# Chunked attention and a quadratic-ReLU FFN: q and k of the first two tiles loaded as eight tokens per row, turned by quarter-array products, and the first loads in another order

## The chip, the cores and the metric

The kernel runs on one core of one Trainium2 chip. The core has five engines with instruction queues of their own: TensorE (PE in the profile, with PEld for its weight loads), VectorE (DVE), ScalarE (ACT), GpSimd (POOL) and SyncE (SP), which here only issues DMAs. Sixteen DMA engines move the data. The metric is the device time of one execution in microseconds; lower is better.

## The reference, cut to what matters

```python
# q, k, v: (8 batches, 8 heads, 576 tokens, 64), float32
q_c = q.reshape(B, H, 9, 64, 64)                     # chunks of 64 tokens, k and v likewise
scores = (1 / sqrt(64)) * q_c @ k_c.transpose(0, 1, 2, 4, 3)
attn = softmax(scores, axis=-1)                      # within each chunk only
out = attn @ v_c                                     # (B, H, S, 64)
x = out.transpose(0, 2, 1, 3).reshape(4608, 512)     # heads side by side
h = x @ w_in                                         # w_in  (512, 2048), float64
g = where(h >= 1, h, where(h <= -1, 0, (h + 1)**2 / 4))
return (g @ w_out).astype(float32)                   # w_out (2048, 512), float64
```

Attention is local to chunks of 64 tokens, so a chunk of a head is a 64 x 64 problem. The weights are float64 in memory.

## The kernel before, in words

The 4608 tokens are nine tiles of 512 (`T`), tile `t`. Eight tiles are the first 512 tokens of a batch; the fifth collects the last 64 tokens of all batches. For each tile there are four head pairs `g` (`NP`), each on 128 partitions, two heads of 64, and 16 blocks `j` (`NF`) of 128 FFN columns.

For a head pair, `load_heads` brings q, k and v; `attn_turn` turns q and k so that the 64 head dimensions lie on partitions; `scores_of` makes 32 products of 64 x 64, each on a quarter of TensorE's array; `attn_softmax` does the softmax on VectorE, ScalarE and, in the first tile, GpSimd; `attn_turn_back` turns the result e; `values_of` makes 32 more quarter products; and `attn_split` writes x into a high and a low part (`xh`, `xl`) for products in a reduced format. Tiles 0 and 1 (`t < FLIPPED`) turn on TensorE: `flip` makes four 128 x 128 transposes into PSUM and ScalarE copies the result out. Later tiles turn on VectorE in blocks of 32.

The FFN makes 12 products per block into h (`ffn_in`, line 554), the activation on ScalarE and VectorE, a split of the result (`ffn_split`) and 12 products back (`ffn_out`, line 589), two blocks later. Each of the 32 weight pieces (`wi` and `wo`, 512 KB each) is loaded once (`load_weight`) and turned from float64 words into a high and a low part by `prepare`: three steps on ScalarE (lines 271, 277, 296) and four on VectorE (lines 274, 281, 286, 300).

The order of the instructions is not that of the calls. Each call adds parts to a `Plan` with an engine, a cost, what it reads and writes, and for DMAs a `lag` and a time `moving`. `Plan.emit` then goes through a modelled time: on each engine, among the parts whose inputs are ready by the model, the part that was added first goes next. Each engine carries out its instructions in that order on the chip and waits where an input is not there. Where TensorE would be idle by the model before the first FFN products, unneeded products with the identity (`warm`, line 704) are put in.

SP issues nearly all loads in the plan's order; the two loads of k for the first two head pairs of tile 0 are issued by ScalarE's queue. `first_loads` (line 619) is the order of the first loads. `load_rows` brings q or k of tiles 0 and 1 in two DMAs of 128 KB, one per head: partition p gets token p of each of the eight chunks, so each piece that is contiguous in memory has 64 floats, 256 bytes. `load_values` brings v in pieces of that size for all tiles.

Of the kernel before, what the change touches and what calls it, by code (L numbers as in the profile page):

```python
# [140 lines left out]
def kernel(  # L141
# [15 lines left out]
    nc = tc.nc  # L157

    B, H, S, D = q.shape
# [3 lines left out]
    C = 64  # L163
    Q = 32
    NP = H // 2
    T = 512
    CT = T // C
    HALF = T // 2
# [137 lines left out]
    def heads_rows(src, t, h):  # L306


        if BATCH[t] is not None:
            return src[BATCH[t], h, :T, :].rearrange("(c p) d -> c p d", p=C)  # L310
        return src[:, h, T:, :]

    def load_rows(dst, src, t, g, queue):

        dst = dst.rearrange("p (c d) -> p c d", d=D)
        for j in range(2):
            queue.dma_start(
                out=dst[j * C:(j + 1) * C],
                in_=heads_rows(src, t, 2 * g + j).rearrange("c p d -> p c d"),
            )  # L320

    def load_blocks(dst, src, t, g, queue):
# [33 lines left out]
    def load_heads(t, g, which="qkv"):  # L356
        for n, src, bufs in (("q", q, q_bufs), ("k", k, k_bufs), ("v", v, v_bufs)):
            if n not in which:
                continue
            key, dst = room(n, bufs, t, g)  # L360
            load = load_values if n == "v" else load_rows if t < FLIPPED else load_blocks
            parts = 4 if load == load_blocks else 2
            if BATCH[t] is None:
                parts *= 2

            issuer, queue = ("act", nc.scalar) if (n, t) == ("k", 0) and g < 2 else ("sp", nc.sync)
            plan.add(
                issuer, 0.67 * parts,
                lambda load=load, dst=dst, src=src, queue=queue: load(dst, src, t, g, queue),
                (), (key,), lag=2.1, moving=2.2 if load == load_blocks else 1.2,  # L370
            )

    def flip(ps, src):
        for u in range(NS):
            cols = slice(u * P, (u + 1) * P)
            nc.tensor.transpose(out=ps[:, cols], in_=src[:, cols], identity=ident)  # L376
# [3 lines left out]
    def attn_turn(t, g):  # L380
        for n, (name, bufs, src_bufs, dst_bufs) in enumerate(
            (("q", "qT", q_bufs, qT_bufs), ("k", "kT", k_bufs, kT_bufs))
        ):
            skey, src = room(name, src_bufs, t, g)
            dkey, dst = room(bufs, dst_bufs, t, g)
            if t >= FLIPPED:
                plan.add("dve", 0.6, lambda src=src, dst=dst: nc.vector.transpose(
                    out=dst, in_=src
                ), (skey,), (dkey,))
                continue  # L390
            pkey, ps = o_banks[n] if t == 0 else a_banks[n]
            plan.add("pe", 0.45, lambda src=src, ps=ps: flip(ps, src), (skey,), (pkey,), columns=T)
            copy = plan.add(
                "act", 0.48, lambda ps=ps, dst=dst: nc.scalar.copy(out=dst, in_=ps),
                (pkey,), (dkey,),
            )
            if t == 0:
                turned[n] = copy

    def scores_of(t, g):  # L400


        qkey, qT = room("qT", qT_bufs, t, g)
        kkey, kT = room("kT", kT_bufs, t, g)
        pkeys, pair = bank_pair_of(t, g)

        def emit():
            for n in range(CT // 2):
                for i in range(2):
                    for half in range(2):  # L410
                        rows = slice(half * C, (half + 1) * C)
                        at = slice((2 * n + i) * C, (2 * n + i + 1) * C)
                        nc.tensor.matmul(  # L413
                            out=pair[i * C:(i + 1) * C, half, n * C:(n + 1) * C],
                            lhsT=qT[rows, at], rhs=kT[rows, at], start=True, stop=True,
                        )

        return emit, (qkey, kkey), pkeys

    def values_of(t, g):  # L420


        akey, aT = room("aT", aT_bufs, t, g)
        vkey, v_sb = room("v", v_bufs, t, g)
        pkeys, pair = bank_pair_of(t, g)

        def emit():
            for n in range(CT // 2):
                for h in range(2):
                    at = (2 * n + h) * C if t < FLIPPED else h * HALF + n * C  # L430
                    of = h * HALF + n * C
                    for half in range(2):
                        rows = slice(half * C, (half + 1) * C)
                        nc.tensor.matmul(  # L434
                            out=pair[h * C:(h + 1) * C, half, HALF + n * C:HALF + (n + 1) * C],
                            lhsT=v_sb[rows, of:of + C], rhs=aT[rows, at:at + C],
                            start=True, stop=True,
                        )

        return emit, (akey, vkey), pkeys  # L440
# [15 lines left out]
    def attn_softmax(t, g):  # L456
        pkeys, pair = bank_pair_of(t, g)
        mkey, mx = room("mx", mx_bufs, t, g)
        skey, sm = room("sm", sm_bufs, t, g)
        ekey, e = room("e", e_bufs, t, g)  # L460
        e3 = e.rearrange("p (n k) -> p n k", k=C)
        e4 = e.rearrange("p (n h k) -> p h n k" if t < FLIPPED else "p (h n k) -> p h n k", h=2, k=C)
        mx4 = mx.rearrange("p (h n) x -> p h n x", h=2)
        sm4 = sm.rearrange("p (n h) x -> p h n x" if t < FLIPPED else "p (h n) x -> p h n x", h=2)
        sc = pair[:, :, :HALF].rearrange("p h (n k) -> p h n k", k=C)

        plan.add("dve", 0.6, lambda: nc.vector.tensor_reduce(  # L467
            out=mx4, in_=sc, axis=AX.X, op=ALU.max
        ), pkeys, (mkey,))
        sums = t == 1  # L470
        if sums:
            plan.add("dve", 0.08, lambda: nc.vector.tensor_scalar_mul(mx, mx, -SCALE), (), (mkey,))

            def exps():
                for n in range(G):
                    nc.scalar.activation(  # L476
                        out=e4[:, n // 4, n % 4, :], in_=sc[:, n // 4, n % 4, :], func=AF.Exp,
                        bias=mx[:, n, :], scale=SCALE, accum_out=sm4[:, n // 4, n % 4, :],
                    )

            plan.add("act", 2.33, exps, (*pkeys, mkey), (ekey, skey))
        else:
            plan.add("dve", 0.6, lambda: nc.vector.tensor_tensor(
                out=e4, in0=sc, in1=mx4.broadcast_to([P, 2, G // 2, C]), op=ALU.subtract
            ), (*pkeys, mkey), (ekey,))
            plan.add("act", 0.52, lambda: nc.scalar.activation(  # L486
                out=e, in_=e, func=AF.Exp, scale=SCALE
            ), (), (ekey,))

        def norm():  # L490
            if not sums:
                nc.vector.tensor_reduce(out=sm, in_=e3, axis=AX.X, op=ALU.add)  # L492
            nc.vector.tensor_scalar_add(sm, sm, 1e-9)
            nc.vector.reciprocal(out=sm, in_=sm)

        plan.add("dve", 0.35 if sums else 1.05, norm, (ekey,), (skey,))
        on_pool = t < 1
        eng = nc.gpsimd if on_pool else nc.vector
        plan.add("pool" if on_pool else "dve", 1.05 if on_pool else 0.6, lambda: eng.tensor_tensor(  # L499
            out=e3, in0=e3, in1=sm.broadcast_to([P, G, C]), op=ALU.mult  # L500
        ), (skey,), (ekey,), port=True)
# [97 lines left out]
    def store(t, s):  # L599
# [16 lines left out]
        plan.add("sp", 0.6, send, (okey,), (), lag=1.7, moving=0.8)  # L616


    first_loads = [
        ("q", 0), ("k", 0), ("q", 1), ("k", 1), ("wi", 0), ("q", 2), ("k", 2), ("v", 0), ("q", 3),  # L620
        ("k", 3), ("v", 1), ("wi", 1), ("v", 2), ("v", 3),
    ]
    for which, n in first_loads:
        if which in ("wi", "wo"):
            load_weight(which, n)
# [4 lines left out]
    for j in range(NF):  # L630
        if j + 2 < NF:
            order.append(("wi", j + 2))
        order.append(("wo", j))
    for g in range(NP + 2):
        if g < NP:
            attn_turn(0, g)
            attn_products(scores_of(0, g))
            attn_softmax(0, g)
        if 1 < g:
            attn_turn_back(0, g - 2)  # L640
            attn_products(values_of(0, g - 2))
            attn_split(0, g - 2)
    loads = [o for o in order if o not in first_loads]

    def load_more(n):
        for _ in range(n):
            if loads:
                load_weight(*loads.pop(0))

    load_more(4)  # L650
    load_heads(1, 0, "qk")
    load_more(2)
    load_heads(1, 0, "v")
    load_more(6)
    load_heads(1, 1)
    prepare("wi", 0)
    prepare("wi", 1)
    prepare("wi", 2)

    LAG = 2  # L660
    todo = order[1:]
# [82 lines left out]
```

## Time and profile before

| | |
|---|---|
| time, median of 3 runs | 868.64 us (868.60 to 869.62) |
| the profiled execution | 869.46 us |
| its span, first to last instruction | 867.7 us |
| mean granted TensorE clock | 0.999 |
| PE, PEld, DVE, ACT busy | 858.8, 706.9, 444.3, 383.1 us |
| bytes moved by DMA | 62.86 MB in 250821 packets, 235904 of them under 512 B |

A row of the timeline gives the start of a group of instructions in microseconds, the time that it covers, the engine, the line of the kernel, the operation, output and inputs, shapes and count; brackets name the idle time of the engine before it and what ended it. "SPq" and "ACTq" rows are DMA issues. The matmul's ends are modelled, so starts are the safer numbers. PE counts as busy with `warm` products too. A table by windows gives the busy time of each engine in stretches of the span.

### The profile page before, as it was taken

What the parts mean: (1) busy time and instruction counts of PE and PEld (TensorE: products, weight loads), DVE (VectorE), ACT (ScalarE), POOL (GpSimd) and SP (SyncE); (2) the same over time, 40 slices, a digit from 0 to 9 for tenths busy, and PEclk for the clock granted to TensorE, in tenths of its full rate; (3) what the DMA queues carried; (4) which work ended last, traced back from release to release, by engine and by line L of the source; (5) the groups of instructions that cost most, each with busy time, mean ns of one, the idle gap of its engine ahead of it and who ended that gap; (6) DMA issues with size and microseconds to landing.
All of it is one profiled execution on the core that took longest, in us unless ns stands there. A gap on an engine that the chain in (4) does not pass through costs nothing.

```text
span 867.7 us, 14916 instructions
## 1 busy us (share of the span) xinstructions
PE 858.8 (99%) x5958; PEld 706.9 (81%) x5958; DVE 444.3 (51%) x762; ACT 383.1 (44%) x703; POOL 4.9 (1%) x10
## 2 busy tenths in 40 slices
PE   9999999999999999999999999999999999999998
PEld 8777788888888888888888888888888888888886
DVE  5999995444544444444544454445444444423222
ACT  5999964333433333333333333333333333333332
POOL 1000000000000000000000000000000000000000
PEclk9999999999999999999999999999999999999999
DMA  9998226322322232222422242223222310001001
GB/s 194 339 316 246 38 39 129 53 46 46 82 48 46 45 85 50 47 49 49 97 50 49 50 93 52 47 46 94 49 39 45 84 28 16 13 1 50 1 0 49
DMA packets 250821, 62.86 MB, mean 72 GB/s; under 512 B 235904, under 2 KB 244096, under 8 KB 250752
## 3 DMA queue, kind: packets, MB, share of 16 engines
q1 hardware_dynamic: 248640, 61.38, 31.5%
q8 instruction: 47, 0.77, 0.4%
q10 hardware_dynamic: 2112, 0.52, 0.3%
q14 instruction: 22, 0.18, 0.1%
HBM read 45.09 MB, written 9.44 MB: 63 GB/s over the span
## 4 chain that ended last, share of the span: by engine, by line
PE 90%; ACT 3%; DVE 2%; issue 1%; DMA 0%; SPq 0%; ACTq 0%; DVEq 0%
PE ps_h L554 43%; PE ps_o L589 43%; PE ps_a L434 2%; PE ps_a L413 2%; ACT tmp L271 1%; DVE tmp L281 0%; ACT parts_wi L296 0%; DVE tmp L286 0%; PE ps_a L376 0%; DMA q_sb<-in_q_dram 0%; ACT words_wi L277 0%; ACT e L476 0%; DVE parts_wo L300 0%; ACT gh L574 0%; ACT r L561 0%
## 5 line engine op out<-in xcount | busy, mean ns | idle before, releaser
L554 PE MATMUL ps_h<-xh,parts_wi 128*128 128x512 f32 x1144 | 381.3, 393 | 0.0
L589 PE MATMUL ps_o<-parts_wo,gh 128*128 128x512 f32 x1152 | 355.3, 390 | 0.0
L589 PEld LDWEIGHTS ps_o<-parts_wo,gh 128*128 128x128 f32 x1152 | 215.9, 188 | 44.8
L554 PEld LDWEIGHTS ps_h<-xh,parts_wi 128*128 128x128 f32 x1144 | 214.8, 188 | 45.9
L565 DVE SCALAR_TENSOR_TENSOR r<-ps_h,r 128x512 f32<-128x512 f32 x143 | 97.3, 681 | 263.2 <-ACT r L564 263.2
L589 PE MATMUL ps_o<-parts_wo,gl 128*128 128x512 f32 x576 | 224.1, 389 | 0.0
L554 PE MATMUL ps_h<-xl,parts_wi 128*128 128x512 f32 x572 | 222.9, 390 | 0.0
L561 ACT ACTIVATE r<-ps_h 128x512 f32<-128x512 f32 x143 | 85.9, 601 | 282.6 <-PE ps_h L554 282.6
L574 ACT CAST gh<-r 128x512 fp32r<-128x512 f32 x144 | 90.2, 626 | 153.3 <-PE ps_o L589 113.1
L575 DVE TENSOR_TENSOR gl<-r,gh 128x512 fp32r<-128x512 f32 x144 | 98.4, 683 | 107.6 <-ACT gh L574 107.6
L589 PEld LDWEIGHTS ps_o<-parts_wo,gl 128*128 128x128 f32 x576 | 108.1, 188 | 22.4
L554 PEld LDWEIGHTS ps_h<-xl,parts_wi 128*128 128x128 f32 x572 | 107.4, 188 | 21.2
L564 ACT ACTIVATE r<-r 128x512 f32<-128x512 f32 x144 | 91.3, 634 | 3.3
L467 DVE TENSOR_REDUCE mx<-ps_a 128x8 f32<-128x512 f32 x34 | 23.4, 688 | 23.1 <-ACT xh L537 13.8
L434 PEld LDWEIGHTS ps_a<-aT,v_sb 64*64 64x64 f32 x1056 | 18.4, 134 | 11.7 <-issue 10.0
L537 ACT CAST xh<-ps_a 128x512 fp32r<-128x512 f32 x34 | 20.0, 589 | 15.0 <-PE ps_a L413 14.5
L492 DVE TENSOR_REDUCE sm<-e 128x8 f32<-128x512 f32 x30 | 20.6, 687 | 10.9 <-ACT e L486 10.9
L434 PE MATMUL ps_a<-aT,v_sb 64*64 64x64 f32 x1056 | 22.9, 224 | 0.1
L538 DVE TENSOR_TENSOR xl<-ps_a,xh 128x512 fp32r<-128x512 f32 x34 | 22.4, 660 | 0.4 <-ACT xh L537 0.4
L499 DVE TENSOR_TENSOR e<-e,sm 128x512 f32<-128x512 f32 x32 | 21.9, 683 | 0.0
L413 PE MATMUL ps_a<-kT,qT 64*64 64x64 f32 x1056 | 21.4, 218 | 0.0
L525 DVE STREAM_TRANSPOSE x<-e 128x512 f32<-128x512 f32 x28 | 19.9, 711 | 0.9
(89 smaller groups left out, 395.4 us busy)
## 6 DMA issues: line engine op xcount, KB each, us to landing
words_wi<-in_moe_w_in_dram SPq DMA_DIRECT2D x16, 512.0 KB, 7.2
words_wo<-in_moe_w_out_dram SPq DMA_DIRECT2D x16, 512.0 KB, 8.6
out_dram<-tmp SPq DMA_DIRECT2D x32, 256.0 KB, 2.5
v_sb<-in_v_dram SPq DMA_DIRECT2D x60, 128.0 KB, 2.6
aT<-x SPq DMA_DIRECT2D x224, 32.0 KB, 1.9
q_sb<-in_q_dram SPq DMA_DIRECT2D x96, 64.0 KB, 2.3
k_sb<-in_k_dram SPq DMA_DIRECT2D x96, 64.0 KB, 2.3
q_sb<-in_q_dram SPq DMA_DIRECT2D x12, 128.0 KB, 8.0
```

What stands on the lines that cost most here:

```text
L413: nc.tensor.matmul(out=pair[i * C:(i + 1) * C, half, n * C:(n + 1) * C], lhsT=qT[rows, at], rhs=kT[rows, at], start=True, stop=True,)
L434: nc.tensor.matmul(out=pair[h * C:(h + 1) * C, half, HALF + n * C:HALF + (n + 1) * C], lhsT=v_sb[rows, of:of + C], rhs=aT[rows, at:at + C] ...
L467: plan.add("dve", 0.6, lambda: nc.vector.tensor_reduce(out=mx4, in_=sc, axis=AX.X, op=ALU.max), pkeys, (mkey,))
L499: plan.add("pool" if on_pool else "dve", 1.05 if on_pool else 0.6, lambda: eng.tensor_tensor(out=e3, in0=e3, in1=sm.broadcast_to([P, G, C] ...
L538: plan.add("dve", 0.6, lambda: nc.vector.tensor_tensor(out=of_tokens(xl), in0=ps, in1=of_tokens(xh.bitcast(F32)), op=ALU.subtract), (*pkey ...
L554: nc.tensor.matmul(out=ps, lhsT=weight["wi", j][:, half, kc * P:(kc + 1) * P], rhs=x, start=(kc == 0 and i == 0), stop=(kc == KC - 1 and i ...
L561: plan.add("act", 0.48, lambda: nc.scalar.activation(out=r, in_=ps, func=AF.Relu, bias=0.5, scale=0.5), (pkey,), (rkey,))
L564: plan.add("act", 0.52, lambda: nc.scalar.square(out=r, in_=r), (), (rkey,))
L565: plan.add("dve", 0.6, lambda: nc.vector.scalar_tensor_tensor(out=r, in0=ps, scalar=1.0, in1=r, op0=ALU.max, op1=ALU.min), (pkey,), (rkey,))
L574: plan.add("act", 0.52, lambda: nc.scalar.copy(out=gh, in_=r), (rkey,), (ghkey,))
L575: plan.add("dve", 0.6, lambda: nc.vector.tensor_tensor(out=gl, in0=r, in1=gh.bitcast(F32), op=ALU.subtract), (rkey, ghkey), (glkey,), port ...
L589: nc.tensor.matmul(out=acc, lhsT=x[:, cols], rhs=weight["wo", j][:, half, :], start=(j == 0 and i == 0), stop=(j == NF - 1 and i == 2),)
```

## The change: what it does

`load_rows` now gives partition p the eight tokens 8p to 8p+7 of a head, one contiguous row of 512 floats, 2 KB. The number of DMAs and their bytes stay. Tokens then lie on the partitions in another order, so `flip_heads` takes the place of `flip` for q and k: for each of the eight tokens r of a row and each of the two heads j, one product of the 64 x 64 block with the identity on a quarter of the array, 16 in place of four 128 x 128 transposes, whose output goes to every eighth column, which puts the tokens back into their order. `flip` stays for e.

For tiles 0 and 1 the scores' blocks are placed as chunks 0, 2, 1, 3 and so on, and e, its sums and the columns that the values products read get the layout of the later tiles.

The plan's time `moving` for these loads goes from 1.2 to 0.75. The first loads come in another order, with wi1 second and wi0 tenth. The loop over the head pairs of tile 0 is written out, in its own sequence, and stands behind three weight loads; the loads of tile 1's first two head pairs and of the following weights are added after the three first preparations, in another sequence.

```diff
     def load_rows(dst, src, t, g, queue):
-        dst = dst.rearrange("p (c d) -> p c d", d=D)
         for j in range(2):
             queue.dma_start(
                 out=dst[j * C:(j + 1) * C],
-                in_=heads_rows(src, t, 2 * g + j).rearrange("c p d -> p c d"),
+                in_=src[BATCH[t], 2 * g + j, :T, :].rearrange("(p r) d -> p (r d)", r=T // C),
             )
...
-                (), (key,), lag=2.1, moving=2.2 if load == load_blocks else 1.2,
+                (), (key,), lag=2.1, moving={load_blocks: 2.2, load_values: 1.2, load_rows: 0.75}[load],
             )
+
+    def flip_heads(ps, src):
+
+        for r in range(T // C):
+            for j in range(2):
+                rows = slice(j * C, (j + 1) * C)
+                nc.tensor.matmul(
+                    out=ps[rows].rearrange("d (p r) -> d r p", r=T // C)[:, r, :],
+                    lhsT=src[rows, r * D:(r + 1) * D], rhs=ident[rows, rows],
+                    start=True, stop=True,
+                )
...
-            plan.add("pe", 0.45, lambda src=src, ps=ps: flip(ps, src), (skey,), (pkey,), columns=T)
+            plan.add("pe", 0.45, lambda src=src, ps=ps: flip_heads(ps, src), (skey,), (pkey,), columns=T)
...
+                    c = 2 * n + i if t >= FLIPPED else n // 2 * 4 + 2 * i + n % 2
...
-                        at = slice((2 * n + i) * C, (2 * n + i + 1) * C)
+                        at = slice(c * C, (c + 1) * C)
...
-                    at = (2 * n + h) * C if t < FLIPPED else h * HALF + n * C
-                    of = h * HALF + n * C
+                    at = h * HALF + n * C
...
-                            lhsT=v_sb[rows, of:of + C], rhs=aT[rows, at:at + C],
+                            lhsT=v_sb[rows, at:at + C], rhs=aT[rows, at:at + C],
...
-        e4 = e.rearrange("p (n h k) -> p h n k" if t < FLIPPED else "p (h n k) -> p h n k", h=2, k=C)
+        e4 = e.rearrange("p (h n k) -> p h n k", h=2, k=C)
...
-        sm4 = sm.rearrange("p (n h) x -> p h n x" if t < FLIPPED else "p (h n) x -> p h n x", h=2)
+        sm4 = sm.rearrange("p (h n) x -> p h n x", h=2)
...
-    first_loads = [
-        ("q", 0), ("k", 0), ("q", 1), ("k", 1), ("wi", 0), ("q", 2), ("k", 2), ("v", 0), ("q", 3),
-        ("k", 3), ("v", 1), ("wi", 1), ("v", 2), ("v", 3),
-    ]
+    first_loads = [("k", 0), ("wi", 1), ("q", 0), ("k", 1), ("q", 2), ("q", 1), ("k", 2), ("k", 3), ("q", 3), ("wi", 0), ("v", 3), ("v", 0), ("v", 1), ("v", 2)]
...
-    for g in range(NP + 2):
-        if g < NP:
-            attn_turn(0, g)
-            attn_products(scores_of(0, g))
-            attn_softmax(0, g)
-        if 1 < g:
-            attn_turn_back(0, g - 2)
-            attn_products(values_of(0, g - 2))
-            attn_split(0, g - 2)
...
-    load_more(4)
-    load_heads(1, 0, "qk")
-    load_more(2)
-    load_heads(1, 0, "v")
-    load_more(6)
-    load_heads(1, 1)
+    load_more(3)
+    attn_turn(0, 0)
+    attn_products(scores_of(0, 0))
+    attn_softmax(0, 0)
...
     prepare("wi", 0)
     prepare("wi", 1)
     prepare("wi", 2)
+    load_more(3)
+    load_heads(1, 0, "qk")
+    load_heads(1, 0, "v")
+    load_heads(1, 1)
+    load_more(6)
```

More of the change, by code (lines that the diff above doesn't have):

```diff
@@ L361, in load_heads @@
             load = load_values if n == "v" else load_rows if t < FLIPPED else load_blocks
-            parts = 4 if load == load_blocks else 2
+            parts = {load_blocks: 4, load_values: 2, load_rows: 2}[load]
             if BATCH[t] is None:
                 parts *= 2
-            issuer, queue = ("act", nc.scalar) if (n, t) == ("k", 0) and g < 2 else ("sp", nc.sync)
+            issuer, queue = ("act", nc.scalar) if (n, g, t) in (("k", 0, 0), ("k", 1, 0)) else ("sp", nc.sync)
             plan.add(
@@ L648, in load_more @@
                 load_weight(*loads.pop(0))
-    load_more(4)
-    load_heads(1, 0, "qk")
-    load_more(2)
-    load_heads(1, 0, "v")
-    load_more(6)
-    load_heads(1, 1)
+    load_more(3)
+    attn_turn(0, 0)
+    attn_products(scores_of(0, 0))
+    attn_softmax(0, 0)
+    attn_turn(0, 1)
+    attn_products(scores_of(0, 1))
+    attn_softmax(0, 1)
+    attn_turn(0, 2)
+    attn_products(scores_of(0, 2))
+    attn_softmax(0, 2)
+    attn_turn_back(0, 0)
+    attn_products(values_of(0, 0))
+    attn_split(0, 0)
+    attn_turn(0, 3)
+    attn_products(scores_of(0, 3))
+    attn_softmax(0, 3)
+    attn_turn_back(0, 1)
+    attn_products(values_of(0, 1))
+    attn_split(0, 1)
+    attn_turn_back(0, 2)
+    attn_products(values_of(0, 2))
+    attn_split(0, 2)
+    attn_turn_back(0, 3)
+    attn_products(values_of(0, 3))
+    attn_split(0, 3)
     prepare("wi", 0)
```

## The prediction

> **What bounds the kernel now.** I read the page's forty slices first, then the busy time by stage, then the timeline of the first 33 us, the waits of TensorE in the stage behind it, and the DMA rates. In the slices each digit is a tenth of about 21.7 us:
>
> ```profile
> PE   9999999999999999999999999999999999999998
> ...
> DVE  5999995444544444444544454445444444423222
> ACT  5999964333433333333333333333333333333332
> ...
> DMA  9998226322322232222422242223222310001001
> ```
>
> PE is called busy all the way, but VectorE, ScalarE and the DMA engines are full only at the head. By stage (columns: stretch, its length, busy us of PE, PEld, DVE, ACT, POOL, then granted clock, DMA share, GB/s):
>
> ```profile
> 0.00:30.00 30.00, 28.40 (x419) 26.15 (x420) 18.93 (x35) 18.29 (x32) 4.89 (x10) 1.00 0.96 227
> 30.00:110.00 80.00, 76.94 (x561) 61.33 (x560) 77.20 (x148) 79.11 (x195) 0.00 (x0) 1.00 0.75 222
> 110.00:860.00 750.00, 750.00 (x4968) 616.89 (x4967) 346.77 (x579) 284.54 (x476) 0.00 (x0) 1.00 0.25 50
> ```
>
> From 110 us on PE has no gap at all, at the full granted clock: nothing there can be won, and the change touches none of it. From 30 to 110 us ACT (79.11 of 80) and DVE (77.20 of 80) prepare the 32 weight pieces and are full, while PE loses 3.06 us. Before 30 us DVE works 18.93 us and sits idle 11.07. So the head is a queue of DVE and ACT work; its end, and with it the end of the kernel, moves by as much as that queue starts earlier. The start of it (columns: start, length):
>
> ```profile
> 0.73 2.78 ACTq L317 DMA_DIRECT2D k_sb<-in_k_dram  x4
> ...
> 0.73 3.06 SPq L317 DMA_DIRECT2D q_sb<-in_q_dram  x4
> ...
> 7.07 0.60 PE L376 MATMUL ps_o<-ident,q_sb 128*128 128x128 f32 x4
> ...
> 7.70 0.59 ACT L394 COPY qT<-ps_o 128x512 f32<-128x512 f32 x1
> 8.49 0.56 PEld L413 LDWEIGHTS ps_a<-kT,qT 64*64 64x64 f32 x32
> ...
> 9.25 0.69 DVE L467 TENSOR_REDUCE mx<-ps_a 128x8 f32<-128x512 f32 x1 [9.25 <-PE ps_a L413]
> ...
> 11.49 0.68 ACT L271 ACTIVATE tmp<-words_wi 128x512 f32<-128x512 f32 x1
> 11.50 2.11 SPq L317 DMA_DIRECT2D first_wi<-in_q_dram  x2
> ...
> 17.50 1.26 DVE L300 TENSOR_TENSOR parts_wi<-tmp,parts_wi 128x512 fp32r<-128x512 f32 x1
> ...
> 23.50 0.48 PE L554 MATMUL ps_h<-xh,parts_wi 128*128 128x512 f32 x1
> ```
>
> DVE's first instruction is at 9.25 us. Of its 11.07 idle us, 9.25 lie before it and 1.82 behind. The chain in front is: q of head pair 0 lands, is turned (7.07), copied (7.70), the scores (8.49), the maximum (9.25). The first product of the FFN comes at 23.50.
>
> **The change part by part.** *The order of work.* The unrolled attention lines add the same parts as the loop, in the same sequence, and the three preparations still come behind them; on PE, ACT, DVE and POOL the planner's tie-breaks are thus those of before. What differs is the queue of SP and the due times of its loads. Layouts of e, the sums, and the columns that scores and values read change addresses, not shapes: no cost, and no cover is needed.
>
> *The loads.* A load of q or k moves as many bytes in the same two DMAs, but in 64 rows of 2 KB each instead of 512 pieces of 256 B. Two stretches bound the rate:
>
> ```profile
> 2.00:7.00 5.00, 5.00 (x29) 5.00 (x28) 0.00 (x0) 1.28 (x1) 0.00 (x0) 1.00 1.14 202
> 22.50:27.50 5.00, 5.00 (x89) 4.25 (x88) 4.71 (x10) 3.82 (x8) 1.09 (x2) 1.00 1.05 384
> ```
>
> In the first the engines are full with 256 B pieces: 202 GB/s. In the second they carry mostly weights in rows of 1 and 4 KB: 384 GB/s. Data begins at about 2.2 us (issue at 0.73 plus 1.5). Before, q0 shares the engines with k0, q1 and k1, four times 0.26 MB, 1.05 MB. After, wi1 (0.52 MB) stands ahead of q0 on SP, and ACT's queue carries k0 and k1: 1.31 MB by the time that q0 is in. At 384 GB/s that is 3.4 us, so q0 lands at 5.65 instead of about 7.05: 1.4 us earlier. At 202 GB/s it would be 6.5 us, landing at 8.7: 1.6 later, for then only the weight in front counts. I take 384, since rows of 2 KB lie between the 1 and 4 KB of that stretch. SP's issue does not bind (columns as in the timeline):
>
> ```profile
> 3.87 0.60 SPq L249 DMA_DIRECT2D words_wi<-in_moe_w_in_dram  x1
> ...
> 8.89 2.56 SPq L348 DMA_DIRECT2D v_sb<-in_v_dram  x2
> ...
> 19.82 1.05 SPq L249 DMA_DIRECT2D words_wi<-in_moe_w_in_dram  x1
> ```
>
> A weight takes 0.60 to issue and four head DMAs 3.06, about 0.65 to 0.77 each without back-pressure; v0's 2.56 for two is back-pressure. So q0 is issued by 2.8, and SP has issued the first list (two weights, ten head loads of two DMAs) by 0.73 + 1.2 + 20 x 0.7 = 16 us, against 19.82 now.
>
> The Trainium skill's page "DMA: Bandwidth & Descriptors" (section "Why small descriptors are slow (HBM only)") gives a fixed overhead of some three cycles per packet, 11 cycles instead of 8 at 256 B. By that, as an estimate, 2 KB rows (67 cycles for 64) would only lift 202 to about 265 GB/s, q0 would land at 7.15, this term would be nothing, and the whole sum 1.4 us smaller. The trace's step from 202 to 384 is larger than that rule alone allows, so I stay with the row.
>
> *The first turning.* Below, a turning costs 0.13 more; two of them stand in the chain, one of them half under a copy: +0.2. The first softmax thus starts at 9.25 - 1.4 + 0.2 = 8.05, gain 1.2.
>
> *wi1 second in the queue.* It lands at about 4.9 (k0, k1 and wi1 are 1.05 MB), so its preparation can use the idle ACT and DVE. One weight's work on DVE:
>
> ```profile
> 27.86 0.68 DVE L281 CUSTOM_DVE_ANT_0 tmp<-words_wi,tmp 128x1024 uint16<-128x1024 uint16 x1
> 28.46 0.69 DVE L300 TENSOR_TENSOR parts_wi<-tmp,parts_wi 128x512 fp32r<-128x512 f32 x1
> 29.06 0.68 DVE L286 SCALAR_TENSOR_TENSOR tmp<-words_wi,tmp 128x512 uint32<-128x512 uint32 x1
> 29.66 0.42 DVE L274 TENSOR_SCALAR tmp<-tmp 128x512 uint32<-128x512 uint32 x1
> ```
>
> By their starts three of them hold DVE 0.60 each and L274 some 0.34: 2.14. After ACT's 0.68 DVE can begin at 5.7; until 8.05 there is room for L274, L281 and L286 (1.54), while L300 must wait for another ACT step. That takes 1.5 us off the queue behind. ACT's own work for it delays q0's copy little, since the turning is not done before 6.2. Of the 1.82 us of later gaps I count 0.3 as gained, because q3 and k3, issued from 11.50 now, are issued by 9.
>
> So the queue starts 1.2 + 1.5 + 0.3 = **3.0 us** earlier. Its bounds: 5.2 (1.2, the whole 2.14, all of 1.82) and 0 (the 202 GB/s case, where the later softmax eats the filled time).
>
> *The turning of tile 1.* It lies among products, where PE's own time may count:
>
> ```profile
> 11.70 1.16 PE L704 MATMUL ps_h<-ident 128*128 128x128 f32 x8
> ...
> 12.69 0.60 PE L376 MATMUL ps_o<-ident,first_wi 128*128 128x128 f32 x4
> ```
>
> ```profile
> 32.36 0.39 PE L554 MATMUL ps_h<-xh,parts_wi 128*128 128x512 f32 x1
> 32.59 0.60 PE L376 MATMUL ps_a<-ident,q_sb 128*128 128x128 f32 x4
> 32.95 0.48 PE L554 MATMUL ps_o<-xh,parts_wi 128*128 128x512 f32 x1
> ...
> 35.81 0.39 PE L554 MATMUL ps_o<-xh,parts_wi 128*128 128x512 f32 x1
> 36.13 0.69 PE L413 MATMUL ps_a<-kT,qT 64*64 64x64 f32 x32
> 36.75 0.50 PE L554 MATMUL ps_o<-xh,parts_wi 128*128 128x512 f32 x1
> ```
>
> Now a turning holds PE 0.36 (32.59 to 32.95). The trace has no quarter-array turning; its nearest row is L413, whose 32 quarter products lie on all four quarters. Eight plain products with the identity take 0.99 from start to start (11.70 to 12.69), 0.124 for 128 columns, so 0.062 for 64. L413's 32 take about 0.5, 0.016 each: a quarter of 0.062, so four run at once. The new turning issues 16 products on two quarters only (rows and outputs of one half each): 8 x 0.062 = 0.49, if these two run side by side. That is +0.13, and in front of L413 PE stands 0.09 longer than the 0.23 between products (32.36 to 32.59): together +0.22, for eight turnings of tile 1 +1.8 us. Bounds: 16 x 0.016 = 0.26 makes it -0.8; all 16 in a row, 0.99, makes it 8 x (0.99 + 0.09 - 0.36) = +5.8. What can hide it are PE's waits in that stage (total, times, longest):
>
> ```profile
> PE ps_a L376 <- DVE e L499: 1.4, 2, 1.0
> PE ps_a L376 <- ACT qT L394: 0.9, 2, 0.6
> ```
>
> A pair's +0.44 is followed by such a wait for another engine that has a queue of its own; some of it, however, runs through the copies into that queue. I charge a quarter of it, **+0.5**. Without this cover it is 1.8.
>
> *What moves later.* q and k of tile 1's first pair go behind wo1, wi4 and wo2. Ahead of them are 1.05 MB of v at 202 GB/s and 6.3 MB of the rest at 384, 21.6 us of transfer, and their own 0.5 MB: they land at 2.2 + 23 = 25 us, against a use at 32.59 - 3 = 29.6. That is free, with 4 us of cover; without it each us is a stall of PE. The load of v for that pair waits for the buffer that the first values product frees; what is queued behind it on SP are weights five and later, not wanted for 20 us.
>
> **Sum.** -3.0 + 0.5 = -2.5 us. The profiled execution took 869.46 us (span 867.7 and 1.76 around it): 866.96. The median of the runs is 868.64, 0.82 below that execution, so the same change gives **866.1 us**. A measurement of this kernel can tell about 0.2%, 1.7 us, from no change.
>
> **The rivals.** *The queue is fuller than I think* (a larger gain): all idle time of DVE that can go goes, 5.2, and the turning hides wholly: 868.64 - 5.2 = 863.4. For it: ACT too is idle 11.7 us before 30, and the weights that follow arrive earlier. Against: the planner's fixed order lets a late step of one chain hold the other.
>
> *wi0 comes too late* (no change): it is now the tenth load, issued near 9.6 and landing near 12; its preparation lasted from 11.49 to 18.76 before. If it again takes 7.3, the first FFN product cannot start before 19.5, which my 20.5 allows; if back-pressure puts the landing at 14.5, it starts at 22 and the softmax work finds DVE's order blocked behind it: I give it -0.4, 868.2.
>
> *The two quarters do not run side by side* (slower): both write the same PSUM bank, whereas L413's two row halves write two banks. A turning then takes 0.99; tile 1 pays 5.8 less at most 3.0 (all PE waits of the stage), and in tile 0 the chain gains 2.0 instead of 3.0. That is +0.8 at best; with half of the cover used, 5.8 - 1.5 - 2.0 = +2.3, 870.9. It decides from about 0.9 us a turning. For it: no row of before shows two row halves on one bank. Against: they write different partitions.
> The Trainium skill's page "TensorEngine Tiling (Array Packing)", section "Restrictions and Gotchas", says that different row tiles cannot use one PSUM bank at the same time; by that rule this rival is the case. No row of before can show it.
>
> **How the numbers follow.** Forecast 0.47 (own range 864.6 to 867.8), larger gain 0.18, no change 0.20, slower 0.15. Faster by over 0.2% (below 866.9): three quarters of the forecast, nearly all of the larger gain, a little of the third: 0.56. Slower (above 870.4): most of the last and a little of the third: 0.14. Within: 0.30. The range goes from the larger gain to the near side of the slower case: 863.0 to 870.6.
>
> **What would show it.** Right: DVE's first instruction is a weight step (L274's successor) near 6 us; first maximum near 8; first FFN product near 20.5; the DMA rate from 2 to 7 us well over 300 GB/s; a turning in tile 1 of some 0.5 us start to start; PE without gaps from about 108. Wrong: a rate near 200; a turning near 1 us; a first product at 22 or later; DVE idle before 30 us still over 10; or new PE waits between 30 and 110 that sum to more than 3 us.

## The result and the profile after

The changed kernel takes 874.23 us (median of 5 runs, 874.13 to 874.29) against 868.75 (5 runs, 868.60 to 869.62) for the one before: a ratio of 1.0059, 95% interval 1.0049 to 1.0070. It is 5.5 us slower, where 2.5 us faster were forecast, and it lies above the predicted range. The profiled execution took 874.23 us with a span of 872.4, at a mean granted clock of 0.999, as before.

The forty slices of the changed kernel (a digit is a tenth of 21.8 us):

```profile
PE   9999999999999999999999999999999999999998
...
DVE  3899997444444444444544454445444444423222
ACT  4899974333433343333433343334333433333332
...
DMA  8996225322222233222422242223222311001001
```

The first digit of VectorE has gone from 5 to 3 and the second of both engines from 9 to 8, and the digit behind the full stretch has risen (VectorE's seventh from 5 to 7, ScalarE's sixth from 6 to 7): the same work comes later. The chain that ended last, by engine:

```profile
PE 99%; DMA 1%; DVE 0%; ACT 0%; ACTq 0%; issue 0%
```

Before, this line of the page read PE 90%, ACT 3%, DVE 2%. On this chain the head is no longer a queue of VectorE and ScalarE work: TensorE itself sets the end from the first turning on. By windows (columns as in the prediction):

```profile
2.00:7.00 5.00, 4.23 (x35) 3.98 (x36) 0.00 (x0) 1.28 (x1) 0.00 (x0) 1.00 1.01 271
0.00:30.00 30.00, 27.88 (x584) 25.76 (x585) 15.68 (x32) 16.23 (x28) 5.16 (x10) 1.00 0.87 255
30.00:110.00 80.00, 80.00 (x811) 64.54 (x810) 73.92 (x142) 76.52 (x190) 0.03 (x1) 1.00 0.70 212
110.00:860.00 750.00, 750.00 (x4968) 616.68 (x4967) 350.77 (x586) 287.13 (x482) 0.00 (x0) 1.00 0.25 50
```

The rate from 2 to 7 us is 271 GB/s, against 202 before and 384 in the sum. VectorE does 15.68 us of work before 30 us, against 18.93. From 30 to 110 us PE has no idle time left (80.00 of 80; 76.94 before), and VectorE now waits (73.92; 77.20 before). The start in the timeline:

```profile
1.25 1.21 SPq L316 DMA_DIRECT2D q_sb<-in_q_dram  x2
...
6.61 1.14 PE L377 MATMUL ps_o<-ident,k_sb 64*64 64x64 f32 x30 [0.77 <-DMA k_sb<-in_k_dram]
...
7.68 1.83 PE L726 MATMUL ps_h<-ident 128*128 128x128 f32 x14
7.78 0.59 ACT L404 COPY kT<-ps_o 128x512 f32<-128x512 f32 x1 [3.08 <-PE ps_o L377]
8.27 0.68 ACT L271 ACTIVATE tmp<-words_wi 128x512 f32<-128x512 f32 x1
...
8.98 0.43 DVE L274 TENSOR_SCALAR tmp<-tmp 128x512 uint32<-128x512 uint32 x1 [8.98 <-ACT tmp L271]
...
9.44 1.15 PE L377 MATMUL ps_o<-ident,q_sb 64*64 64x64 f32 x32
...
12.85 0.69 DVE L477 TENSOR_REDUCE mx<-ps_a 128x8 f32<-128x512 f32 x1 [1.89 <-PE ps_a L424]
...
25.04 0.48 PE L564 MATMUL ps_h<-xh,parts_wi 128*128 128x512 f32 x1
```

VectorE's first instruction is the weight step L274, as predicted, but at 8.98 instead of 5.7. The first maximum is at 12.85 instead of 8.05, and the first FFN product at 25.04 instead of 20.5 (23.50 before). The turning of q0 at 9.44 does not follow its data, which had landed at 7.4 (its second DMA was issued at 1.88 and took 5.5 us to land); seven unneeded products (14 rows of L726) stand between it and the turning of k0.

Two turnings in tile 1:

```profile
36.86 0.39 PE L564 MATMUL ps_o<-xh,parts_wi 128*128 128x512 f32 x1
37.18 1.15 PE L377 MATMUL ps_a<-ident,q_sb 64*64 64x64 f32 x32
38.16 1.10 PE L377 MATMUL ps_a<-ident,k_sb 64*64 64x64 f32 x32
39.19 0.50 PE L564 MATMUL ps_o<-xh,parts_wi 128*128 128x512 f32 x1
...
40.78 0.69 PE L424 MATMUL ps_a<-kT,qT 64*64 64x64 f32 x32
41.41 0.50 PE L564 MATMUL ps_h<-xh,parts_wi 128*128 128x512 f32 x1
```

They hold PE from 37.18 to 39.19, 1.0 us each. The prediction had 0.49, and the transposes took 0.36. The count at the end of the row tells why: `flip_heads` issues 16 products, and the row shows 32. So does `scores_of`, whose loops (4 x 2 x 2) make 16 products and not the 32 that the text ahead of the prediction gives them (and `values_of`): the row L424 x32 is 16 products as well. A float32 product runs as two passes in this trace.

### The profile page after: what moved, and what is told of

The parts are those of the page before. It is cut to its first block, busy times and chain, and to the rows that moved or that the text cites. A ratio compares the mean times of both kernels' runs of the same rounds, so it can differ in the third digit from the quotient of the medians.

```text
span 872.4 us, 15789 instructions
## 1 busy us (share of the span) xinstructions
PE 866.1 (99%) x6394; PEld 713.5 (82%) x6394; DVE 443.1 (51%) x762; ACT 382.9 (44%) x703; POOL 5.2 (1%) x10
## 3 DMA queue, kind: packets, MB, share of 16 engines
HBM read 45.09 MB, written 9.44 MB: 62 GB/s over the span
## 4 chain that ended last, share of the span: by engine, by line
PE 99%; DMA 1%; DVE 0%; ACT 0%; ACTq 0%; issue 0%
PE ps_h L564 45%; PE ps_o L599 45%; PE ps_a L444 2%; PE ps_a L424 2%; PE ps_a L377 1%; PE ps_o L377 1%; PE ps_h L726 1%; DMA k_sb<-in_k_dram 1%; PE ps_o L564 0%; PE ps_o L386 0%; PE ps_a L386 0%; PE ps_o L726 0%; PE ps_o L444 0%; PE ps_o L424 0%; DVE tmp L613 0%; ACT tmp L615 0%
## 5 line engine op out<-in xcount | busy, mean ns | idle before, releaser
L509 DVE TENSOR_TENSOR e<-e,sm 128x512 f32<-128x512 f32 x32 | 21.8, 682 | 0.0
L424 PE MATMUL ps_a<-kT,qT 64*64 64x64 f32 x1056 | 21.5, 218 | 0.0
```

Source lines behind the costliest of these rows:

```text
L424: nc.tensor.matmul(out=pair[i * C:(i + 1) * C, half, n * C:(n + 1) * C], lhsT=qT[rows, at], rhs=kT[rows, at], start=True, stop=True,)
```

## The experiments

The kernel before ran beside each group of experiments, at medians of 868.57 to 869.07 us. Ratios are to it, with 95% intervals.

**The turning alone taken back.** The new loads, layouts and order stay; tokens stay in the order in which they were loaded.

```diff
-lambda src=src, ps=ps: flip_heads(ps, src)
+lambda src=src, ps=ps: flip(ps, src)
```

> The changed kernel with its loads, its order and its planner's costs, but q and k of both tiles turned by the four 128 x 128 transposes of before, in the same places of TensorE's order. Left out: the right placing of tokens and heads, so scores are those of other tokens; all shapes and counts behind the turning stay. Theory A (the turnings cost: 1.08 us of TensorE each where a transpose group took 0.36 to 0.44, sixteen of them, in a TensorE order that is one unbroken chain from 6.6 us on): 16 x 0.69 = 11 us leave TensorE, of which some 3 us come back as waits for ScalarE and VectorE between 30 and 110 us; 864 to 868 us, first FFN product near 21 us. Theory B (the new order of loads costs: q0 and k0 late behind wi1): the late start stays, 871 to 874 us, first FFN product after 24 us.

Measured: 867.27 us (10 runs), 0.9983 (0.9974 to 0.9993). Windows and two rows of its timeline:

```profile
0.00:30.00 30.00, 27.51 (x404) 24.32 (x405) 18.65 (x38) 18.68 (x33) 5.19 (x10) 1.00 0.93 263
30.00:110.00 80.00, 78.07 (x570) 63.12 (x571) 77.27 (x148) 78.69 (x195) 0.00 (x0) 1.00 0.71 211
```

```profile
11.16 0.69 DVE L477 TENSOR_REDUCE mx<-ps_a 128x8 f32<-128x512 f32 x1 [0.35 <-PE ps_a L424]
...
21.73 0.48 PE L564 MATMUL ps_h<-xh,parts_wi 128*128 128x512 f32 x1
```

The planner's order is that of the changed kernel, its 45 unneeded products included; only the turnings are shorter. The first FFN product comes 3.3 us earlier (21.73 against 25.04), PE has idle time again from 30 to 110 (1.93), and VectorE and ScalarE are full there. The turnings cost 7.0 us (874.23 - 867.27), more than the whole loss; theory A held.

**Tile 1 back to before.** Loads in 256 B pieces, transposes and the old layouts for tile 1; tile 0 as changed.

```diff
-load = load_values if n == "v" else load_rows if t < FLIPPED else load_blocks
+load = load_values if n == "v" else load_rows if t == 0 else load_rows_old if t < FLIPPED else load_blocks
...
-lambda src=src, ps=ps: flip_heads(ps, src)
+lambda src=src, ps=ps: (flip_heads if t == 0 else flip)(ps, src)
```

> The changed kernel with tile 1 as before: its q and k in 256 byte pieces, transposes, and the layouts that go with them; tile 0 and the order of loads as changed. Theory A: eight turnings give 8 x 0.69 = 5.5 us back to TensorE between 30 and 110 us, less up to 3 us of waits that come back: 869 to 872 us, first FFN product unchanged at about 25 us. Theory B: no more than 1 us, 873 to 874.5.

Measured: 871.79 us (5 runs), 1.0036 (1.0021 to 1.0050), with the first FFN product at 25.12, as theory A had it.

```profile
30.00:110.00 80.00, 77.67 (x598) 62.14 (x597) 76.73 (x147) 78.91 (x195) 0.11 (x1) 1.00 0.72 211
```

Tile 1's turnings cost 2.4 us of the whole (874.23 - 871.79). PE's idle time is back (2.33). That fits the rows: eight turnings longer by 1.0 - 0.36 are 5.1 us, and 3.06 us of PE's waits were there to take them up, which leaves 2.1. The rest, 871.79 - 867.27 = 4.5 us, is tile 0's (with tile 1's pieces of 256 B in it).

**The order of the loads alone.** The kernel before, with the new list of first loads and the new sequence behind it.

```diff
-    first_loads = [
-        ("q", 0), ("k", 0), ("q", 1), ("k", 1), ("wi", 0), ("q", 2), ("k", 2), ("v", 0), ("q", 3),
...
+    first_loads = [("k", 0), ("wi", 1), ("q", 0), ("k", 1), ("q", 2), ("q", 1), ("k", 2), ("k", 3), ("q", 3), ("wi", 0), ("v", 3), ("v", 0), ("v", 1), ("v", 2)]
```

> The kernel before with the changed order of first loads and of the loads added later, everything else as before (256 byte pieces, transposes, moving 1.2). Theory A: no part of the loss: 866 to 870 us. Theory B: the whole loss: 872 to 876 us, with the first maximum on VectorE at 11 us or later in place of 9.25.

Measured: 870.37 us (10 runs), 1.0020 (1.0010 to 1.0029), between the ranges of the two theories.

```profile
2.00:7.00 5.00, 4.01 (x23) 3.82 (x22) 0.00 (x0) 1.28 (x1) 0.00 (x0) 1.00 1.17 247
```

The first maximum is at 12.32 (9.25 before), the first FFN product at 24.51 (23.50 before). With 256 B pieces the new order alone loses 0.2%. Two things can have made this. The weight ahead of q0 makes it land at 7.5 instead of 6.9 us. And the plan, given the other order, puts in 61 unneeded products instead of 51; of their rows, which follow each other at 0.111 us, 82 instead of 68 stand between the first turning and the first FFN product, 14 x 0.111 = 1.6 us. The runs do not tell the two apart.

**Rows and products under the old order.** The changed kernel with the first loads and the sequence of the kernel before.

```diff
-    first_loads = [("k", 0), ("wi", 1), ("q", 0), ("k", 1), ("q", 2), ...
+    first_loads = [
+        ("q", 0), ("k", 0), ("q", 1), ("k", 1), ("wi", 0), ("q", 2), ("k", 2), ("v", 0), ("q", 3),
```

> The changed kernel with the order of loads of before: rows of 2 KB, the quarter products and moving 0.75 stay. Theory A: the whole loss stays: 872 to 876 us. Theory B: it is gone: 867 to 869 us.

Measured: 878.46 us (4 runs, 877.26 to 882.01), 1.0121 (1.0097 to 1.0145), above the ranges of both theories; the first maximum is at 10.65 and the first FFN product at 26.52. Windows and waits of PE from 30 to 110 us:

```profile
30.00:110.00 80.00, 77.68 (x805) 63.04 (x804) 73.69 (x141) 75.11 (x188) 0.00 (x0) 1.00 0.73 218
```

```profile
PE ps_a L386 <- DVE e L509: 2.1, 1, 2.1
```

Here PE is not full in that stage, and a wait of 2.1 us for VectorE is left. Against the next experiment, which has the same order and transposes, the products cost 9.5 us (878.46 - 868.94); under the new order they cost 7.0. Where the other 2.5 us come from was not followed.

**Rows and transposes under the old order.** The first experiment with the old lists.

```diff
-lambda src=src, ps=ps: flip_heads(ps, src)
+lambda src=src, ps=ps: flip(ps, src)
...
-    first_loads = [("k", 0), ("wi", 1), ("q", 0), ("k", 1), ("q", 2), ...
+    first_loads = [
+        ("q", 0), ("k", 0), ("q", 1), ("k", 1), ("wi", 0), ("q", 2), ("k", 2), ("v", 0), ("q", 3),
```

> As e1_transposes (rows of 2 KB for both tiles, moving 0.75, the four 128 x 128 transposes in place of the quarter products, so tokens and heads are mixed), with the order of loads of before. It completes the square of order and rows at the old turning. Theory D1 (the rows' faster landing is worth the same 3.1 us under either order, as between e3_order_only and e1_transposes): 865 to 866.5 us. Rival D2 (rows pay only together with the new order, since under the old one the planner's order, not the landing, holds the first chain): 868 to 871 us. The DMA rate from 2 to 7 us should be 250 GB/s or more under both.

Measured: 868.94 us (10 runs), 1.0006 (0.9996 to 1.0016).

```profile
2.00:7.00 5.00, 4.74 (x28) 4.53 (x28) 0.00 (x0) 1.86 (x2) 0.00 (x0) 1.00 0.91 237
```

```profile
9.07 0.69 DVE L477 TENSOR_REDUCE mx<-ps_a 128x8 f32<-128x512 f32 x1 [9.07 <-PE ps_a L424]
...
22.61 0.48 PE L564 MATMUL ps_h<-xh,parts_wi 128*128 128x512 f32 x1
```

The rate rises to 237 GB/s only, the first maximum comes 0.18 us earlier than before, and the time does not move. The change of the loads thus brings nothing under the old order, and 870.37 - 867.27 = 3.1 us under the new one: the times are those of D2. That the rows themselves make the 3.1 us is not shown. The plan's `moving` goes from 1.2 to 0.75 with them, and under the new order the plan then puts in 45 unneeded products instead of 61. That is 50 of their rows instead of 82 between the first turning and the first FFN product, 32 x 0.111 = 3.6 us, while q0 lands at 7.5 in both kernels. Under the old order their number stays (50 against 51). The first FFN product is 0.9 us earlier here without a gain in the time; ten rows fewer stand ahead of it than before (58 against 68) and ten more behind it (20 against 10), which fits.

**One quarter after the other.** The two loops of `flip_heads` exchanged, so that eight products of one half run before the eight of the other.

```diff
-        for r in range(T // C):
-            for j in range(2):
+        for j in range(2):
+            for r in range(T // C):
```

> The changed kernel with the two loops of the turning exchanged: first the eight products of one head, all on one quarter of the array, then the eight of the other. Results and counts are the same. Theory B1 (two quarters run side by side when they alternate, and a quarter takes one product at a time, 64 columns in two passes of 0.062 us): a turning takes 2.0 us instead of 1.08, and the kernel 880 to 890 us. Rival B2 (TensorE looks far enough ahead, or the two never ran side by side): 1.0 to 1.1 us a turning, 873.5 to 875 us.

Measured: 884.92 us (2 runs), 1.0186 (1.0165 to 1.0206). Two turnings in its tile 1:

```profile
42.09 1.72 PE L377 MATMUL ps_a<-ident,q_sb 64*64 64x64 f32 x29
...
43.82 1.67 PE L377 MATMUL ps_a<-ident,k_sb 64*64 64x64 f32 x29
...
45.42 0.50 PE L564 MATMUL ps_o<-xh,parts_wi 128*128 128x512 f32 x1
```

3.33 us for the two, 1.67 each, against 1.0 with the quarters in turn. The single records of the traces show why. On one quarter a pass of 64 columns starts every 0.058 us (here from 42.19 to 42.83). In the changed kernel the passes start in pairs, 0.007 us apart, one pair every 0.058 us (37.29 to 39.04), and in L424 in fours, again every 0.058 us. So two quarters take no longer for a pair than one for a single pass: they run side by side, on one PSUM bank. Theory B1 held, in the time as well; its 2.0 us for a turning is too high, because the second half starts before the last passes of the first.

**The planner's cost put right.** The plan still books 0.45 us for a turning.

```diff
-plan.add("pe", 0.45, lambda src=src, ps=ps: flip_heads(ps, src), (skey,), (pkey,), columns=T)
+plan.add("pe", 1.05, lambda src=src, ps=ps: flip_heads(ps, src), (skey,), (pkey,), columns=T)
```

> The changed kernel with one number put right: the planner is told 1.05 us for a turning by quarter products instead of 0.45. Its order then holds 15 warm products ahead of the first FFN products instead of over 40. Theory A1 (beside the turnings' own time, warm products that the planner put into idle time that no longer exists stand in TensorE's unbroken chain, some 62 passes of 0.124 us, 7.7 us, after 6.6 us): part of this comes back, up to where ScalarE, VectorE and the loads hold the chain; first FFN product at 22 to 24 us, 870 to 873 us. Theory A2 (only the turnings' own time counts; the warm products merely fill waits): 873.5 to 875 us.

Measured: 886.17 us (4 runs), 1.0207 (1.0190 to 1.0224). Both theories missed it. Its windows from 20 us (the granted clock is the third number from the end):

```profile
20.00:22.00 2.00, 0.81 (x28) 0.67 (x24) 1.90 (x6) 0.25 (x1) 1.26 (x1) 1.00 0.98 265
22.00:24.00 2.00, 0.69 (x32) 0.56 (x32) 1.20 (x3) 1.49 (x3) 0.05 (x1) 0.90 0.99 347
24.00:26.00 2.00, 0.75 (x28) 0.75 (x32) 1.84 (x4) 2.00 (x5) 1.05 (x1) 0.50 1.06 394
26.00:28.00 2.00, 2.00 (x22) 1.53 (x15) 2.00 (x5) 2.00 (x5) 0.00 (x0) 0.50 1.06 392
28.00:30.00 2.00, 1.28 (x4) 0.59 (x4) 2.00 (x5) 2.00 (x4) 0.00 (x0) 0.50 1.05 355
```

With the larger cost the model sees TensorE busy and puts in 15 unneeded products in place of 45. TensorE is then busy for 0.7 to 0.8 of 2 us, and the granted clock falls to 0.50 from about 24 us, just ahead of the first FFN product (27.08).

**The same for tile 0 alone**, on the kernel with tile 1 as before.

```diff
-plan.add("pe", 0.45, ...
+plan.add("pe", 1.05 if t == 0 else 0.45, ...
```

> As e2_tile1_back (tile 1 as before, tile 0 by rows of 2 KB and quarter products), with the planner's cost for tile 0's turnings at 1.05 us. Theory A1: the eight turnings of tile 0 then take the place of warm products instead of standing beside them: 866.5 to 869.5 us. Theory A2: as e2_tile1_back, 871 to 872 us.

Measured: 880.34 us (4 runs), 1.0132 (1.0117 to 1.0147), 8.6 us more than with the false cost (871.79) and above both theories. The plan puts in 15 unneeded products here as well, and the clock falls:

```profile
16.00:18.00 2.00, 0.66 (x4) 0.42 (x4) 0.77 (x2) 1.48 (x3) 0.57 (x1) 0.95 0.58 130
18.00:20.00 2.00, 1.73 (x48) 1.73 (x50) 1.97 (x4) 1.66 (x4) 0.00 (x0) 0.50 0.95 215
```

**Two orders of the first loads**, on that kernel: q0 directly behind k0, and the sequence of before.

```diff
-first_loads = [("k", 0), ("wi", 1), ("q", 0), ("k", 1), ...
+first_loads = [("k", 0), ("q", 0), ("k", 1), ("wi", 1), ("q", 1), ("q", 2), ("k", 2), ("k", 3), ("q", 3), ("wi", 0), ("v", 0), ...
```

> As e9_tile0_cost, with the first loads k0, q0, k1, wi1, q1, q2, k2, k3, q3, wi0, v0 to v3: the first q no longer stands behind a weight. If the weight in front is what the order costs: first maximum on VectorE at 8 to 9.5 us and 1 to 2 us below e9_tile0_cost. If not: within 0.7 us of it.

```diff
-first_loads = [("k", 0), ("wi", 1), ("q", 0), ("k", 1), ...
+first_loads = [("k", 0), ("q", 0), ("k", 1), ("q", 1), ("wi", 0), ("q", 2), ("k", 2), ("v", 0), ("q", 3), ("k", 3), ("v", 1), ("wi", 1), ...
```

> As e9_tile0_cost, with the sequence of first loads of before (k0 added ahead of q0, v and wi as there); the loads added later keep the changed sequence. If the early weight preparation is worth its place: 0.5 to 2 us above e11_q0_first. If not: equal to it within 0.7 us.

Measured: 885.56 us (4 runs), 1.0192 (1.0175 to 1.0209), and 879.51 (4 runs), 1.0123 (1.0108 to 1.0138). The first maximum is at 10.74 and 11.51, earlier than the 12.14 of the kernel that they start from. Neither expectation holds. The plan puts in 14 and 12 unneeded products here, against 15, and the clock fell by different amounts in the three (means before 30 us of 0.87, 0.89 and 0.85), so these two say nothing about q0's place.

**The right cost, and the unneeded products kept.** The plan counts `columns` in steps of 3.41 us and books products at half speed after a step with fewer than 3072 (`products_end`). Four times as many columns for a turning keep its model at full speed; TensorE then seems idle more often, and 32 fillers are put in.

```diff
-plan.add("pe", 0.45, ..., columns=T)
+plan.add("pe", 1.05, ..., columns=4 * T)
```

> The changed kernel with the turning's cost at 1.05 us in the planner, as e5_cost, and its columns at 2048 instead of 512, so that the planner does not take TensorE for half as fast while it turns. Its order then has 32 warm products ahead of the FFN, between the 15 of e5_cost and the 45 of the changed kernel. Theory A3 (the warm products hold the clock, which fell to 0.5 in e5_cost; where they stand in real gaps they cost nothing): the granted clock stays at 1.00 and the time is 871 to 874.5 us. Rival A4 (quarter products by themselves let the clock fall, or the longer cost spoils the order): clock below 0.97 again between 20 and 40 us and 878 us or more.

Measured: 875.48 us (4 runs), 1.0085 (1.0065 to 1.0106). The time lies between the two theories. In the profiled execution, which took 879.03 us where the other three took 874.85 to 875.65, the mean clock is 0.91 between 20 and 40 us, against 0.66 with the larger cost alone: the dip is shorter but not gone. For tile 0 alone, with tile 1 as before:

```diff
-plan.add("pe", 0.45, ..., columns=T)
+plan.add("pe", 1.05 if t == 0 else 0.45, ..., columns=4 * T if t == 0 else T)
```

> As e9_tile0_cost (tile 1 as before, tile 0 by rows of 2 KB and quarter products at 1.05 us in the planner) with 2048 columns per turning of tile 0. Theory A3: clock at 1.00, 868 to 872 us, not above e2_tile1_back's 871.8 by more than 0.5. Rival A4: clock below 0.97 before 40 us, 876 us or more.

Measured: 870.03 us (10 runs), 1.0015 (1.0005 to 1.0024). That is 1.8 us better than the false cost (871.79) and 10.3 better than 15 fillers (880.34), and still not faster than the kernel before. A3's time held, but not its clock: in the profiled execution (871.15 us, more than the median) TensorE stands idle from 16 to 18 us, the clock falls to 0.50 after that, and a window ahead of the first FFN product (26.88) still shows the dip:

```profile
20.00:25.00 5.00, 5.00 (x139) 4.50 (x138) 3.59 (x9) 3.32 (x7) 1.04 (x1) 0.87 1.03 313
```

## Why the prediction was wrong

*The sum.* From the runs, as differences of medians: the new order +1.6 (870.37 against 868.73), the rows and the plan's time for them under it -3.1, the turnings +7.0; together +5.5. The prediction's terms were -3.0 for the first two and +0.5 for the third. Loads and order, with what the plan made of them, did gain, 1.5 us, about half of the term. The split depends on the way that is taken: under the old order the rows bring nothing, the turnings cost 9.5, and the new order then gains 4.2 (878.46 - 874.23). Either way the step that turned the sign is the turning.

*The turning of tile 1: "16 products on two quarters only ... 8 x 0.062 = 0.49".* The 0.062 was a half of 0.124, the distance from one row to the next (0.111 in the single records), which was taken for the time of a product. A float32 product is two rows, in L704 as in L413. With 32 rows for 16 products the same working gives 32 x 0.062 / 2 = 0.99, and 1.0 was measured. The four transposes of before are four rows, and the scores' 16 products 32, so reading the count beside the loops would have shown it. The size was wrong by 0.5 us, sixteen times.

*"I charge a quarter".* With the true size the cover was too small: 5.1 us against 3.06. All of it was used (PE 80.00 of 80), and 2.4 us were left over. Whether a quarter would have been right for the small size was not tested.

*"The two quarters do not run side by side."* This rival had the right price for a turning (0.99) and a wrong reason. The exchange of the loops shows that they do, 1.0 against 1.67 us, and a pair of passes every 0.058 us, as one alone. So the rule of the Trainium skill's page "TensorEngine Tiling (Array Packing)", section "Restrictions and Gotchas", that different row tiles cannot use one PSUM bank at once, is not borne out by these rows. Its 870.9 us was too low because it charged 1.0 us in tile 0 (4.5 measured) and kept a gain of 3.0 for loads and order (1.5 measured); for tile 1 it charged 4.3, more than the 2.4 measured.

*"The first turning ... two of them stand in the chain ... +0.2".* This overlooked that in tile 0 the chain runs through TensorE itself. The chain of waits of the changed kernel begins so:

```profile
1.32 5.25 DMA k_sb<-in_k_dram
6.61 1.14 PE ps_o L377 x30
7.75 1.76 PE ps_h L726 x14
9.51 1.08 PE ps_o L377 x32
10.58 0.64 PE ps_h L726 x4
11.22 1.01 PE ps_o L377 x29
```

From 6.61 on there is no gap: turnings and unneeded products follow each other. The products that fill TensorE before 30 us (busy, mean ns of one, idle before):

```profile
L726 PE MATMUL ps_h<-ident 128*128 128x128 f32 x78 | 12.6, 311 | 1.4 <-POOL ident masks.py:199 1.4
...
L726 PE MATMUL ps_o<-ident 128*128 128x128 f32 x6 | 0.8, 274 | 0.0
```

With six more rows of ps_o from 33.7 us on they are 90 rows, two for each of the 45 products. Of these, 22 lie before the first turning, 50 between it and the first FFN product, 5.6 us at 0.111 each, and 18 behind. The fillers themselves are not new: the kernel before has 51, with 68 rows in that place. But they were put where the plan, which books 0.45 us for a turning, saw TensorE idle; on the chip that time was taken by the turnings. All eight turnings of tile 0 therefore count: 8 x (1.0 - 0.36) = 5.1 us, of which 3.3 show at the first FFN product and some 4.5 in the time. The prediction named this order as fixed only in a rival, and did not add up TensorE's own work before 25 us.

*"I take 384, since rows of 2 KB lie between".* 271 GB/s were measured (266 and 272 in the two first experiments, with the same loads of tile 0), and q0 landed at 7.4 us, not at 5.65: 0.5 later than before (6.9), where 1.4 earlier was forecast. The row of another stretch did not carry over. The estimate of 265, worked out from the Trainium skill's page "DMA: Bandwidth & Descriptors", section "Why small descriptors are slow (HBM only)", came near, but in part by luck: it was for the rows alone, and for them the runs show a smaller step in this stretch, from 247 to 266 under the new order (the third and the first experiment) and from 202 to 237 under the old. The rest came with the new order. k0, with wi1 beside it on the engines, landed only at 6.57 (the first row of the chain above).

*"After ACT's 0.68 DVE can begin at 5.7".* The step was there, at 8.98. In ScalarE's order the copy of k0 (7.78), which waited for k0 and its turning, stands before wi1's first step (8.27), although wi1 had landed at 5.6 (issued at 0.74, 4.9 us to landing). The prediction asked only how little wi1's step would delay the copy of q0; it was the copy of k0 that delayed wi1.

*Right:* the loads of tile 1 that moved behind weights cost nothing (the first q was issued at 23.34, landed less than 9 us later and was turned at 37.18, with no gap on TensorE), and from 110 us on TensorE works without a gap as before.

## What to carry to other kernels

Hold the count in a row against the loops of the code before a duration per product is taken from it: a factor of two hid there, and it decided the sign. Where an order is written by a planner's costs, a new operation booked at its old cost makes the plan fill time that is no longer free; but before that cost is put right, look at what the fillers do for the clock. A change of an order or of a planner's time also changes its fillers: count them before a gain or a loss is put down to the loads. And a higher rate is not an earlier landing of the piece that is waited for: here 271 GB/s came in place of 202, and q0 landed at 7.4 us in place of 6.9.

## What the runs showed of the hardware

Not expected: the granted clock fell to 0.50 when the unneeded products went from 45 to 15 and TensorE was busy 0.66 to 0.81 of 2 us in the windows ahead of it; with 32 of them it fell as low but for less time in the one profiled execution of each kernel (means of 0.91 and 0.97 from 20 to 40 us, against 0.66 and 0.63 with 15), with 45 not at all. The kernels with 15 take 8.6 us (tile 0's cost alone) and 11.9 us (both tiles, 886.17 - 874.23) longer than those with 45. How much work holds the clock was not measured, nor what part of these times is the clock's and what part the other order's. Also new: float32 products run as two passes while transposes run as one, and two quarters that write one PSUM bank run side by side, a pair of passes every 0.058 us, as one pass on a single quarter.
